# A speech joint network, forward and backward: operations recorded with reads and writes and issued by an in-kernel list scheduler; a shorter gelu'; row form of fe by DMA transpose

## The chip, the cores and the metric

One Trainium2 chip, one of its cores. The core has TensorE (PE; its weight loads are listed as PEld), VectorE (DVE), ScalarE (ACT), GpSimd (POOL) and SyncE (SP), which run their instructions in order and wait for each other by semaphores, and 16 DMA engines. SP issues all DMA transposes here; POOL issues the large loads and stores. The metric is the device time of the program in microseconds, the median of several runs.

## The reference, cut to what matters

```python
B, T, D, K, U = 2, 16000, 256, 3, 8
def _fwd_reference(x, w1, w2, g, w_f, w_g, w_o):
    xp = jnp.pad(x, ((0,0),(pad,pad),(0,0)))
    for i in range(K):
        h = h + jnp.einsum("btc,cd->btd", xp[:, i:i+T, :], w1[i])
    h = _gelu(h)[:, ::2, :]
...
    for i in range(K):
        f = f + jnp.einsum("btc,cd->btd", hp[:, i:i+T1, :], w2[i])
    f = _gelu(f)[:, ::2, :]
    fe = jnp.einsum("btd,de->bte", f, w_f)
    ge = jnp.einsum("bud,de->bue", g, w_g)
    j = jnp.tanh(fe[:, :, None, :] + ge[:, None, :, :])
    return jnp.einsum("btud,dv->btuv", j, w_o)
```

All is bfloat16, gelu is the tanh form. The outputs are this result (2 x 4,000 x 8 x 256) and the gradients of all seven inputs for a given `grad_out`.

## The kernel before

Of every four time steps of x the strided convolutions keep one of f, so the kernel works on 4,000 positions of each of two batches, in 18 chunks: 14 of 512 positions, two of 256 and two of 160. Channels lie on the 128 partitions in two halves; the four phases of x come transposed from HBM as tiles XC.

Each chunk goes through three stages, and the main loop runs stage j of chunk k beside stage a of chunk k+1 and stage de of chunk k-1:

- *Stage a* (`stage_a`): two convolutions give h at odd and even steps (HTo, HTe), a third gives f (FT). Each keeps its gelu' (G1o, G1e, G2) for the backward pass. `conv_gelu` does the six matmuls of each channel half, `gelu_half` lets ACT take the square and the gelu out of PSUM and DVE form g_s; `gelu_grad` forms gelu' with one ACT tanh and six DVE passes (lines 231 to 237). HTo is also written by DVE with the last column of the chunk before (line 274, from HTo_halo); there is one buffer of HTo. Then DMA transposes on SP make the row forms HRo, HRs, HRe and FR; fe is computed twice on PE, with channels on partitions (FE, line 309) and with positions on partitions (FER, line 322), both copied by ACT.
- *Stage j* (`stage_j`): for each pair of the eight u, ACT forms JT, the tanh of FE plus a column of GE (line 340). PE multiplies JT by WO (line 433), ACT copies the result to OUT_SB and POOL stores it. PE multiplies the transposed grad_out (GOT) by WO transposed (line 399), DVE multiplies by 1 - JT squared (JSQ, NGZ, line 411) and adds over u (ZS, line 417). The row form of the same tanh (JR: DVE adds FER and GEB, line 376; ACT, line 424) is multiplied by rows of grad_out (GO_R) into GWO_ps (line 353).
- *Stage de* (`stage_de`): backward through w_f, w2 and w1 (GF, GHo, GHe), their row forms by PE transposes and copies, the weight gradients (line 545, added to ACC by DVE, line 482), and the gradient of x (line 576), copied by ACT to GX_SB (three buffers) and stored by POOL (line 586).

Stages are generators; the main loop steps them by fixed fractions, and the framework's own scheduler gives the final order. PSUM has two pools, four banks for stage j (psj) and three for a and de (psa). Most copies out of PSUM have their engine written in the code, ACT for OUT_SB and GX_SB.

Of the kernel before, what the change touches and what calls it, by code (L numbers as in the profile page):

```python
# [17 lines left out]
GELU_A = float(2.0 * np.sqrt(2.0 / np.pi))  # L18


@with_exitstack
def kernel(
# [29 lines left out]

    CW = 512
    UP = U // 2
    full = [CW] * ((MQ - 2 * P) // CW)
# [9 lines left out]
    NG = len(chunks)  # L65

    const = ctx.enter_context(tc.tile_pool(name="const", bufs=1))
    accp = ctx.enter_context(tc.tile_pool(name="accp", bufs=1))
    xcp = ctx.enter_context(tc.tile_pool(name="xcp", bufs=7))
    htp = ctx.enter_context(tc.tile_pool(name="htp", bufs=2))  # L70
    keep = ctx.enter_context(tc.tile_pool(name="keep", bufs=3))
    fep = ctx.enter_context(tc.tile_pool(name="fep", bufs=1))
    gel = ctx.enter_context(tc.tile_pool(name="gel", bufs=2))
    jtp = ctx.enter_context(tc.tile_pool(name="jtp", bufs=3))
    gop = ctx.enter_context(tc.tile_pool(name="gop", bufs=3))
    jop = ctx.enter_context(tc.tile_pool(name="jop", bufs=2))
    jrp = ctx.enter_context(tc.tile_pool(name="jrp", bufs=3))
    keep2 = ctx.enter_context(tc.tile_pool(name="keep2", bufs=2))
    jzp = ctx.enter_context(tc.tile_pool(name="jzp", bufs=4))
    dep = ctx.enter_context(tc.tile_pool(name="dep", bufs=1))  # L80
    dep2 = ctx.enter_context(tc.tile_pool(name="dep2", bufs=2))
    x5p = ctx.enter_context(tc.tile_pool(name="x5p", bufs=4))
    gxp = ctx.enter_context(tc.tile_pool(name="gxp", bufs=3))
    psG = ctx.enter_context(tc.tile_pool(name="psG", bufs=1, space=bass.MemoryType.PSUM))
    psJ = ctx.enter_context(tc.tile_pool(name="psJ", bufs=4, space=bass.MemoryType.PSUM))
    psA = ctx.enter_context(tc.tile_pool(name="psA", bufs=3, space=bass.MemoryType.PSUM))

    def ps_j(dt=FP32):
        return psJ.tile([P, CW if dt == FP32 else 2 * CW], dt, name="psj" if dt == FP32 else "psjb", tag="psj")

    def ps_a(dt=FP32):
        return psA.tile([P, CW if dt == FP32 else 2 * CW], dt, name="psa" if dt == FP32 else "psab", tag="psa")

    def after(later, earlier, sync=True):

        cls = mybir.DependencyClass.Sync if sync else mybir.DependencyClass.NoSync
        tc.add_manual_dep(later.ins, earlier.ins.name, mybir.DependencyInfo(cls, mybir.DependencyReason.DATA),
                          reason="order of the first loads")

    xq = x.rearrange("b (q four) d -> b four q d", four=4)  # L100

    def load_xc(g_):
        b, ci, c0, W = chunks[g_]
        tiles = []
        for c in (1, 2, 3, 0):
            XC = xcp.tile([P, KT, CW + 16], BF16, name="XC")
            if c == 3 and ci > 0:
                nc.sync.dma_start_transpose(out=XC[:, :, 0:16 + W], in_=xq[b, c, c0 - 16:c0 + W, :])
            else:
                if c == 3:  # L110
                    nc.vector.memset(XC[:, :, 0:16], 0.0)
                nc.sync.dma_start_transpose(out=XC[:, :, 16:16 + W], in_=xq[b, c, c0:c0 + W, :])
            tiles.append(XC)
        return {1: tiles[0], 2: tiles[1], 3: tiles[2], 0: tiles[3]}

    def load_got(g_, up):
        b, ci, c0, W = chunks[g_]
        GOT = gop.tile([P, 2, KT, CW], BF16, name="GOT")
        for j in range(2):
            nc.sync.dma_start_transpose(out=GOT[:, j, :, :W], in_=grad_out[b, c0:c0 + W, 2 * up + j, :])  # L120
        return GOT

    def load_gor(g_, up):
        b, ci, c0, W = chunks[g_]
        GO = gop.tile([P, CW // P, 2, V], BF16, name="GO_R")
        nb, rem = W // P, W % P
        src = grad_out[b, c0:c0 + W, 2 * up:2 * up + 2, :].rearrange("t u v -> t (u v)")
        if nb:
            i_ = nc.gpsimd.dma_start(out=GO[:, 0:nb].rearrange("p a u v -> p a (u v)"),  # L129
                                     in_=src[0:nb * P].rearrange("(a p) n -> p a n", p=P))  # L130
            if g_ == 0:
                late.append(i_)
        if rem:
            nc.gpsimd.dma_start(out=GO[:rem, nb].rearrange("p u v -> p (u v)"), in_=src[nb * P:W])
        return GO

    ident = const.tile([P, P], BF16, name="ident")
    make_identity(nc, ident[:])
    W1 = const.tile([P, KK, KT, D], BF16, name="W1")
    xc_tiles = {0: load_xc(0)}  # L140
    for i in range(KK):
        nc.scalar.dma_start(out=W1[:, i], in_=w1[i].rearrange("(kt p) n -> p kt n", p=P))
    W2 = const.tile([P, KK, KT, D], BF16, name="W2")
    WF = const.tile([P, KT, D], BF16, name="WF")
# [23 lines left out]

    gTs = []

    def make_geb(b):

        for u2 in range(UP):
            ps = ps_j()
# [439 lines left out]
    for _ in gen:  # L614
        pass
# [106 lines left out]
```

## Time and profile before

| | |
|---|---|
| runs (3), median | 927.06 us (925.51 to 930.01) |
| profiled execution, span from first to last instruction | 926.7 us |
| TensorE clock, mean granted | 0.974 |
| DMA moved | 173.21 MB, mean 187 GB/s |

The profiled execution is told by its span; no other time of it is given. Its span lies 0.4 us below the median of the runs. In the profile a row of a group gives the line, engine, operation, output and inputs, shape and count; behind the bar the busy time in us, the mean ns of one, and the idle time of the engine just before them with what ended it. In the timeline a row begins with start and length in us, and idle time stands in brackets with its releaser. One name can stand for a helper: the copies of many tiles are all line 205 (ACT) or 207 (DVE).

### The profile page before, as it was taken

How to read it: one execution, taken by the hardware profiler on the slowest of the kernel's cores; microseconds unless marked ns; L12 is line 12 of the kernel's file. 1: busy time of each engine (PE TensorE's matmuls, PEld its weight loads, DVE VectorE, ACT ScalarE, POOL GpSimd, SP SyncE). 2: the span in 40 equal slices, each digit the busy share in tenths (PEclk: the TensorE clock that was granted, in tenths of full speed). 3: DMA queues.
4: the chain of work that ended last, by engine and by line, in shares of the span. 5: the costliest groups of instructions: out<-in, count | busy, mean ns of one | idle time of the engine just before them, and what ended most of it. 6: DMA issues, size and time to landing. Idle time of an engine off the chain costs nothing.

```text
span 926.7 us, 17730 instructions
## 1 busy us (share of the span) xinstructions
PE 854.3 (92%) x6396; PEld 598.7 (65%) x6396; DVE 776.6 (84%) x1807; ACT 745.6 (80%) x1271; POOL 207.2 (22%) x376
## 2 busy tenths in 40 slices
PE   5758999999999999999999999999999989899997
PEld 3434656767575766767675657576675747678873
DVE  2676999797988969897979899897979879798783
ACT  2777997979889797978697888979797897978752
POOL 2102211213122121313231212122131211214240
PEclk8888999999999999999999999999999999999997
DMA  8799998877878787785989886998887787837542
GB/s 185 124 193 217 205 239 166 241 174 208 207 178 215 169 215 174 208 204 176 187 194 213 194 189 157 233 185 228 166 230 181 163 202 173 222 109 216 144 127 67
DMA packets 308056, 173.21 MB, mean 187 GB/s; under 512 B 279648, under 2 KB 283776, under 8 KB 307968
## 3 DMA queue, kind: packets, MB, share of 16 engines
q1 hardware_dynamic: 276944, 68.48, 43.5%
q0 software_dynamic: 29152, 102.69, 34.2%
q10 hardware_dynamic: 1872, 0.92, 0.5%
q8 instruction: 50, 0.82, 0.4%
q14 instruction: 38, 0.31, 0.1%
HBM read 54.44 MB, written 50.34 MB: 113 GB/s over the span
## 4 chain that ended last, share of the span: by engine, by line
ACT 30%; PE 29%; DVE 15%; issue 15%; DMA 6%; SPq 2%; POOL 2%; ACTq 0%; POOLq 0%; DVEq 0%
ACT JT L340 9%; PE psa L545 7%; ACT JR L424 5%; ACT OUT_SB L205 5%; PE psa L576 4%; PE GWO_ps L353 4%; DMA out_dram<-GX_SB 3%; PE psj L433 3%; ACT JSQ L408 3%; PE psj L399 3%; PE psa L248 3%; DVE NGZ L411 2%; DVE ZS L417 2%; ACT g_sq L225 2%; ACT g_s L231 1%
## 5 line engine op out<-in xcount | busy, mean ns | idle before, releaser
L205 ACT CAST OUT_SB<-psj 128x512 bf16<-128x512 f32 (+1 forms) x256 | 156.9, 614 | 43.7 <-PE psj L433 43.7
L340 ACT ACTIVATE JT<-FE,GE 128x512 bf16<-128x512 f32 (+2 forms) x288 | 186.1, 700 | 0.0
L433 PE MATMUL psj<-WO,JT 128*128 128x256 bf16 (+1 forms) x1024 | 162.4, 274 | 11.3 <-ACT OUT_SB L205 10.2
L399 PE MATMUL psj<-GOT,WOT 128*128 128x512 bf16 (+2 forms) x576 | 159.8, 357 | 9.6 <-DMA GOT<-in_grad_out_dram 9.3
L411 DVE SCALAR_TENSOR_TENSOR NGZ<-JSQ,psj 128x512 f32<-128x512 bf16 (+2 forms) x252 | 152.6, 613 | 16.1 <-PE psj L399 15.9
L424 ACT ACTIVATE JR<-JR 128x1024 bf16<-128x1024 bf16 (+2 forms) x136 | 140.9, 1039 | 10.7 <-DVE JR L376 10.7
L353 PE MATMUL GWO_ps<-GO_R,JR 128*128 128x256 bf16 (+1 forms) x1024 | 144.7, 274 | 5.1 <-ACT JR L424 4.1
L433 PEld LDWEIGHTS <-JT 128*128 128x128 bf16 (+1 forms) x1024 | 99.3, 98 | 71.6 <-issue 21.0
L417 DVE TENSOR_TENSOR ZS<-ZS,NGZ 128x512 f32<-128x512 f32 (+2 forms) x216 | 131.9, 617 | 0.6
L444 POOL DMA_DIRECT2D out_dram<-OUT_SB x72 | 52.9, 735 | 315.8 <-ACT OUT_SB L205 301.5
L353 PEld LDWEIGHTS <-JR 128*128 128x128 bf16 (+1 forms) x1024 | 98.0, 98 | 30.9 <-ACT JR L424 10.4
L225 ACT ACTIVATE g_sq<-psa 128x512 bf16<-128x512 f32 (+2 forms) x106 | 60.4, 570 | 64.8 <-PE psa L248 60.7
L248 PE MATMUL psa<-XC,W 128*128 128x512 bf16 (+2 forms) x420 | 94.1, 357 | 11.9 <-DVE g_s L227 11.5
L248 PEld LDWEIGHTS <-W 128*128 128x128 bf16 x648 | 62.5, 99 | 60.9 <-issue 17.4
L482 DVE TENSOR_TENSOR ACC_GW<-ACC_GW,psa 128x512 f32<-128x512 f32 x96 | 65.6, 686 | 41.1 <-PE psa L545 41.1
L376 DVE TENSOR_TENSOR JR<-FER,GEB 128x1024 bf16<-128x1024 bf16 (+2 forms) x136 | 88.8, 657 | 9.9 <-PE GWO_ps L353 9.8
L205 ACT CAST GX_SB<-psa 128x512 bf16<-128x512 f32 (+1 forms) x128 | 76.0, 633 | 21.6 <-DMA out_dram<-GX_SB 14.3
L227 DVE SCALAR_TENSOR_TENSOR g_s<-g_sq,psa 128x512 bf16<-128x512 bf16 (+2 forms) x106 | 65.5, 618 | 29.9 <-ACT HTo L226 27.0
L545 PEld LDWEIGHTS <-X 128*128 128x128 bf16 (+1 forms) x768 | 75.0, 98 | 16.4 <-issue 3.7
L129 POOL DMA_DIRECT2D GO_R<-in_grad_out_dram x72 | 52.5, 730 | 123.7 <-PE GWO_ps L353 108.4
L399 PEld LDWEIGHTS <-WOT 128*128 128x128 bf16 x576 | 55.1, 99 | 31.3 <-DMA GOT<-in_grad_out_dram 9.9
L576 PE MATMUL psa<-W1T,GHo 128*128 128x256 bf16 (+1 forms) x384 | 74.6, 277 | 0.3
(138 smaller groups left out, 1474.8 us busy)
## 6 DMA issues: line engine op xcount, KB each, us to landing
GO_R<-in_grad_out_dram POOLq DMA_DIRECT2D x56, 512.0 KB, 5.1
out_dram<-OUT_SB POOLq DMA_DIRECT2D x56, 512.0 KB, 4.3
X<-in_x_dram POOLq DMA_DIRECT2D x60, 320.0 KB, 4.3
out_dram<-GX_SB POOLq DMA_DIRECT2D x60, 256.0 KB, 3.9
GOT<-in_grad_out_dram SPq DMA_TRANSPOSE x144, 4.7
GO_R<-in_grad_out_dram POOLq DMA_DIRECT2D x8, 256.0 KB, 5.0
out_dram<-OUT_SB POOLq DMA_DIRECT2D x8, 256.0 KB, 4.5
XC<-in_x_dram SPq DMA_TRANSPOSE x72, 4.0
```

What stands on the lines that cost most here:

```text
L205: nc.scalar.copy(out=out, in_=in_)
L248: mm = nc.tensor.matmul(ps[:, :W], lhsT=w[:, mt * P:(mt + 1) * P], rhs=rhs, start=(k == 0), stop=(k == len(mms) - 1))
L340: nc.scalar.activation(out=JT[:, j, mt, :W], in_=st[g_]["FE"][mt][:, :W], func=ACT.Tanh, bias=GE[:, b, mt, 2 * up + j:2 * up + j + 1], sca ...
L353: nc.tensor.matmul(GWO_ps[:, dt, :], lhsT=JR[:m, tb % 2, j, dt * P:(dt + 1) * P], rhs=GO[:m, tb, j, :], start=(n == 0), stop=(n == n_gwo - 1))
L376: nc.vector.tensor_tensor(out=JR[:m, lo % 2:lo % 2 + n], in0=st[g_]["FER"][:m, lo:hi].unsqueeze(2).to_broadcast([m, n, 2, D]), in1=GEB[:m, ...
L399: mm = nc.tensor.matmul(gj[:, :W], lhsT=WOT[:, kt, dt * P:(dt + 1) * P], rhs=GOT[:, j, kt, :W], start=(kt == 0), stop=(kt == KT - 1))
L411: nc.vector.scalar_tensor_tensor(out=NGZ[:, :W], in0=JSQ[:, dt, :W], scalar=1.0, in1=gj[:, :W], op0=ALU.subtract, op1=ALU.mult, accum_out= ...
L417: nc.vector.tensor_tensor(out=S["NGFE"][:, dt, :W] if fin_ else ZS[:, dt, :W], in0=ZS[:, dt, :W], in1=NGZ[:, :W], op=ALU.add)
L424: nc.scalar.activation(out=dst, in_=dst, func=ACT.Tanh)
L433: nc.tensor.matmul(ps[:m, jj * V:(jj + 1) * V], lhsT=JT[:, jj, kt, tb * P:tb * P + m], rhs=WO[:, kt, :], start=(kt == 0), stop=(kt == KT - 1))
L545: nc.tensor.matmul(ps[:, dt * D:(dt + 1) * D], lhsT=lhs(bl, m, dt), rhs=rhs[:m, bl, :], start=(k == 0), stop=(k == n - 1))
L576: nc.tensor.matmul(ps[:m, cj * D:(cj + 1) * D], lhsT=l_, rhs=r_, start=(k == 0), stop=(k == len(mms) - 1))
```

## The change

Operations are no longer issued as the code runs. Each is recorded by `op` with its engine (or a choice of ACT and DVE), a cost in ns, the buffers that it reads and writes and a place in the intended sequence; at the end `issue` simulates the engines with these costs and issues the operation that can start first, and among equals the one with the lowest place. The framework keeps that order (`manual_schedule`). With it:

- all seven PSUM banks of the two pools are one pool; a buffer is given to the operation that starts first. HTo, GF, NGFE, the row tiles and FE have two buffers (FE is bfloat16), XC six instead of seven;
- copies out of PSUM (OUT_SB, GX_SB, FE, row forms, GEB) and JSQ go to ACT or DVE, whichever the plan finds free first;
- what is kept is gelu' - 1 = (1 - t) (c (3 q + 1) h - 1/2) instead of gelu' (t the tanh, q the scaled square, h the gelu): five DVE passes instead of six, two products instead of three tensor-tensor passes; its users add the 1 in a `scalar_tensor_tensor`. GF no longer takes a factor of -1; the sign is undone where GX is copied and the weight gradients are stored;
- FER is no longer a matmul: SP transposes FE by DMA;
- the halo columns of HTo and G1o are copied by POOL, without the small HTo_halo tile;
- W2 comes in three loads, and the loads of the head are no longer held back to the first matmuls by explicit dependences.

```diff
+    WAKE = {"PE": 45.0, "ACT": 25.0, "DVE": 25.0, "POOL": 280.0, "SP": 60.0}
+    TAIL = {"PE": 180.0, "ACT": 130.0, "DVE": 95.0, "POOL": 40.0, "SP": 0.0}
...
+    def issue(self):
...
+                for o in lst:
+                    s = o.ready + wake
+                    for b in o.new:
...
+                        s = max(s, f + wake)
...
+                    k = (max(s, t), o.prio, o, e)
+                    if cand is None or k < cand:
+                        cand = k
+                if cand is not None and (best is None or cand[0] < best[0]):
+                    best = cand
...
+            T[e] = s + o.cost[o.eng.index(e)]
+            if o.work:
+                dma_free = max(dma_free, T[e] - 400.0) + o.work
+                o.done = dma_free + 2000.0
+            else:
+                o.done = T[e] + self.TAIL[e]
+            o.fn(e)
...
+def c_pe(ns):
+    return sum(max(n / 2.4 + 2.5, 25.0) for n in ns)
+def c_act(n, psum=False, ptr=False):
+    return (50.0 if psum else 93.0) + (92.0 if ptr else 0.0) + 0.833 * n
+def c_dve(n, f=1.0):
+    return 66.0 + 1.042 * n * f
...
-    psJ = ctx.enter_context(tc.tile_pool(name="psJ", bufs=4, space=bass.MemoryType.PSUM))
-    psA = ctx.enter_context(tc.tile_pool(name="psA", bufs=3, space=bass.MemoryType.PSUM))
+    F.cls("ps", 7, any_order=True, psum=True)
...
-        nc.vector.tensor_scalar(out=sq, in0=sq, scalar1=3.0, scalar2=1.0, op0=ALU.mult, op1=ALU.add)
-        nc.vector.tensor_scalar(out=om, in0=th, scalar1=-c, scalar2=c, op0=ALU.mult, op1=ALU.add)
-        nc.vector.tensor_tensor(out=om, in0=om, in1=sq, op=ALU.mult)
-        nc.vector.tensor_tensor(out=om, in0=om, in1=h, op=ALU.mult)
-        nc.vector.tensor_scalar(out=th, in0=th, scalar1=0.5, scalar2=0.5, op0=ALU.mult, op1=ALU.add)
-        nc.vector.tensor_tensor(out=gp_out, in0=om, in1=th, op=ALU.add)
+            out=sq[:, :, :W], in0=sq[:, :, :W], scalar1=3.0 * c, scalar2=c, op0=ALU.mult, op1=ALU.add),
+            out=sq[:, :, :W], in0=sq[:, :, :W], in1=h_ap(None), op=ALU.mult), r=[sq, (h_buf, 0), (h_buf, 1)], w=[sq], at=late)
+            out=sq[:, :, :W], in0=sq[:, :, :W], scalar1=-0.5, scalar2=None, op0=ALU.add), r=[sq], w=[sq], at=late)
+            out=s[:, :, :W], in0=s[:, :, :W], scalar1=-1.0, scalar2=1.0, op0=ALU.mult, op1=ALU.add),
+            out=g_ap(), in0=s[:, :, :W], in1=sq[:, :, :W], op=ALU.mult), r=[s, sq], w=[(g_buf, 0), (g_buf, 1)], at=late)
...
-                    nc.tensor.matmul(ps[:m, (bl % 2) * D:(bl % 2 + 1) * D], lhsT=FT[:, kt, bl * P:bl * P + m],
-                                     rhs=WF[:, kt, :], start=(kt == 0), stop=(kt == KT - 1))
+            dma("SP", lambda kt=kt: FER[:, 0:Wp // P, kt * P:(kt + 1) * P], lambda kt=kt: FE[:, kt, 0:Wp],
+                r=[(FE, kt), (FE, "z")], w=[(FER, kt)], bytes_=Wp * P * 2, new=[FER] if kt == 0 else [], transpose=True)
...
-            nc.vector.tensor_copy(out=HTo[:, :, 1:2], in_=pv["HTo_halo"][:])
+            op("POOL", 200.0, lambda e: nc.gpsimd.tensor_copy(out=HTo[:, :, 1:2], in_=pv["HTo"][:, :, pw + 1:pw + 2]),
...
+    ctx.enter_context(tc.manual_schedule())
+    F.issue()
```

What the order becomes, at three places. The first is ACT in a full chunk in the middle, from the copy of the last FE to the next chunk's row tanh JR. Before:

```order
L205 COPY FE_4079<-psa 128x512
L205 COPY FE_4084<-psa 128x512
L205 CAST OUT_SB<-psj 128x512
L408 ACTIVATE JSQ<-JT 128x1024
L205 CAST GX_SB<-psa 128x512
L205 CAST FER<-psa 128x512
L205 CAST OUT_SB<-psj 128x512
L205 CAST FER<-psa 128x512
L340 ACTIVATE JT<-FE_4079,GE 128x512
L205 CAST GX_SB<-psa 128x512 x3
L424 ACTIVATE JR<-JR 128x1024
```

And in the change:

```order
L276 CAST FE<-ps 128x512 x2
L517 ACTIVATE JT<-FE,GE 128x512 x2
L276 CAST OUT_SB<-ps 128x512
L517 ACTIVATE JT<-FE,GE 128x512 x3
L276 CAST OUT_SB<-ps 128x512
L517 ACTIVATE JT<-FE,GE 128x512
L565 ACTIVATE JSQ<-JT 128x1024
L517 ACTIVATE JT<-FE,GE 128x512 x2
L276 CAST OUT_SB<-ps 128x512 x2
L565 ACTIVATE JSQ<-JT 128x1024
L535 ACTIVATE JR<-JR 128x1024 x2
```

The FER copies are gone, eight tanh of JT stand ahead of the first JR, and some copies of GX_SB and OUT_SB of this stretch are on DVE. The second place is SP at the end of stage a of a full chunk: HR and FR are row forms for the weight gradients, GOT the transposed grad_out. Before:

```order
L301 DMA_TRANSPOSE FR<-FT 128x4x128
L301 DMA_TRANSPOSE HRe<-HTe 128x4x128 x2
L301 DMA_TRANSPOSE HRs<-HTo 128x4x128 x2
L301 DMA_TRANSPOSE HRo<-HTo 128x4x128 x2
L301 DMA_TRANSPOSE FR<-FT 128x4x128
L120 DMA_TRANSPOSE GOT<-in_grad_out_dram 128x2x512 x4
```

And in the change:

```order
L291 DMA_TRANSPOSE GOT<-in_grad_out_dram 128x2x512
L291 DMA_TRANSPOSE FR<-FT 128x4x128
L291 DMA_TRANSPOSE GOT<-in_grad_out_dram 128x2x512
L291 DMA_TRANSPOSE FER<-FE 128x4x128
L291 DMA_TRANSPOSE FR<-FT 128x4x128
L291 DMA_TRANSPOSE GOT<-in_grad_out_dram 128x2x512
L291 DMA_TRANSPOSE FER<-FE 128x4x128
L291 DMA_TRANSPOSE GOT<-in_grad_out_dram 128x2x512 x2
```

The two FER transposes stand each behind a load of GOT, where the loads of a group stood together. The third is POOL near the end of stage de of a full chunk; GX_SB holds the gradient of x, GHe_halo one column for the next chunk. Before:

```order
L533 COPY GHe_halo<-GHe 128x2
L444 DMA out_dram<-OUT_SB 128x4x512
L129 DMA GO_R<-in_grad_out_dram 128x4x512
L444 DMA out_dram<-OUT_SB 128x4x512
L586 DMA out_dram<-GX_SB 128x1024 x3
```

And in the change:

```order
L722 COPY GHe_halo<-GHe 128x2
L293 DMA out_dram<-OUT_SB 128x4x512
L293 DMA GO_R<-in_grad_out_dram 128x4x512
L293 DMA out_dram<-GX_SB 128x1024 x2
L293 DMA out_dram<-OUT_SB 128x4x512
L293 DMA out_dram<-GX_SB 128x1024 x2
```

Two stores of GX_SB moved ahead of the store of OUT_SB that all of them stood behind.

1169 lines of the change are left out of this document (670 added, 499 removed).

## The prediction

> **What bounds the kernel now.** I read the page's first part, then the stretches of the span, then the matmul groups by shape, and last single waits in the chain of waits and the timeline.
>
> ```profile
> PE 854.3 (92%) x6396; PEld 598.7 (65%) x6396; DVE 776.6 (84%) x1807; ACT 745.6 (80%) x1271; POOL 207.2 (22%) x376
> 430.24 3.49 PE psa L545 x32
> 176.91 1.29 PE psa L248 x6
> L433 PE MATMUL psj<-WO,JT 128*128 128x256 bf16 x992 | 157.2, 274 | 11.3 <-ACT OUT_SB L205 10.2 <-DVE NGZ L411 0.2
> ...
> L186 PE MATMUL psab<-ident,GR 8*128 8x8 bf16 x4 | 0.4, 173 | 3.3 <-DMA GR<-in_g_dram 3.3
> ```
>
> TensorE is the bound, but 92% says too much: a mean of 274 ns overlaps its successor. Where nothing waits, 32 matmuls of 256 columns take 3.49 us, 109 ns each, and six of 512 columns 1.29 us, 216 ns each. That is columns / 2.4 + 2.5 ns. Put on all shapes of the list (its first row and its last are shown), the 6,396 matmuls need **794.1 us**, a mean of 0.1242 us. Weight loads hide behind them. The execution's span is 926.7 us, so 132.6 us are lost; the stretches say where.
>
> ```profile
> 0.00:25.00 25.00, 12.27 (x76) 8.70 (x77) 6.08 (x24) 6.26 (x16) 6.92 (x19) 0.81 0.84 174
> 25.00:50.00 25.00, 19.16 (x112) 11.65 (x112) 18.21 (x52) 18.74 (x37) 2.94 (x4) 0.85 0.82 149
> 50.00:75.00 25.00, 17.07 (x89) 10.02 (x89) 17.69 (x52) 18.52 (x33) 5.14 (x8) 0.80 0.96 186
> 75.00:100.00 25.00, 18.84 (x122) 11.71 (x120) 19.19 (x42) 21.03 (x34) 3.87 (x6) 0.93 1.11 214
> 100.00:150.00 50.00, 46.66 (x333) 31.29 (x332) 48.65 (x105) 44.43 (x72) 9.35 (x16) 1.00 1.00 219
> 600.00:700.00 100.00, 96.26 (x733) 68.59 (x732) 86.84 (x185) 84.78 (x136) 21.44 (x37) 1.00 0.86 202
> 900.00:927.00 27.00, 22.01 (x128) 11.36 (x125) 9.73 (x30) 6.60 (x14) 2.08 (x4) 0.74 0.20 58
> ```
>
> A row gives a stretch's length, busy time and count of PE, weight loads, DVE, ACT and POOL, then the granted clock, the DMA share and GB/s. The first 100 us hold 399 matmuls, worth 49.5 us: 50.5 lost, in the **head**. The last 27 us hold 128, worth 15.9: 11.1 lost, in the **tail**. The 800 us between hold 5,869, worth 728.9: **71.1 lost in the middle**, 9%.
>
> In the middle PE stands mostly for an accumulator buffer that ACT or DVE has not emptied yet:
>
> ```profile
> PE psa L248 <- DVE g_s L227: 11.9, 11, 1.4
> PE psj L433 <- ACT OUT_SB L205: 10.2, 13, 1.6
> PEld L353 <- ACT JR L424: 10.4, 16, 2.1
> ...
> 741.17 2.55 ACT L340 ACTIVATE JT<-FE,GE 128x512 bf16<-128x512 f32 x4
> 743.72 0.47 ACT OUT_SB L205
> 738.91 0.94 ACT JSQ L408
> 744.25 0.60 PE L433 MATMUL psj<-WO,JT 128*128 128x256 bf16 x4 [1.57 <-ACT OUT_SB L205]
> ```
>
> The first three are rows of waits (total, times, longest), the others of the timeline and of the chain. At 742 us PE wants a buffer whose evacuation stands on ACT behind four tanh; PE loses 1.57 us. So it goes once in most chunks: 11 + 13 such waits, 22.1 us. That is a matter of order, not of load.
>
> **The change part by part.** *Work.* The row form of fe was 128 matmuls:
>
> ```profile
> L322 PE MATMUL psa<-WF,FT 128*128 128x256 bf16 x124 | 19.0, 278 | 0.6
> L234 DVE TENSOR_TENSOR g_om<-g_om,g_sq 128x1024 bf16<-128x1024 bf16 x42 | 28.9, 688 | 0.0
> 752.32 0.68 DVE L227 SCALAR_TENSOR_TENSOR g_s<-g_sq,psa 128x512 bf16<-128x512 bf16 x1
> 752.92 0.69 DVE L417 TENSOR_TENSOR ZS<-ZS,NGZ 128x512 f32<-128x512 f32 x1
> L205 ACT CAST FER<-psa 128x512 bf16<-128x512 f32 x30 | 18.9, 638 | 0.7 <-PE psa L322 0.7
> FR<-FT SPq DMA_TRANSPOSE x36, 2.9
> GOT<-in_grad_out_dram SPq DMA_TRANSPOSE x144, 4.7
> 21.39 2.48 SPq L301 DMA_TRANSPOSE HRo<-HTo  x2
> q1 hardware_dynamic: 276944, 68.48, 43.5%
> q0 software_dynamic: 29152, 102.69, 34.2%
> HBM read 54.44 MB, written 50.34 MB: 113 GB/s over the span
> ```
>
> 128 x 0.109 = **14.0 us off PE**, leaving 780.1. DVE instructions follow each other every 0.60 us. The shorter gelu' drops one product in each of 54 places, 42 of them 1024 wide: 42 x 0.60 + 12 x some 0.3 = 29 us. The counts of the changed order give it other work back: 51 GX and 46 full OUT evacuations come to DVE (97 x 0.60 = 58 us), while 39 of the large JSQ squares go to ACT (23 us less), ten large row copies as well (6 us less). With the rest, DVE stays where it is within 5 us. ACT loses the FER copies (15 us) and those 97 evacuations at 0.47 each (46 us), and takes 39 squares at 0.94 (37 us) and ten row copies (10 us): some 14 us less. So no engine gets heavier; neither DVE nor ACT ends later than PE, and their savings by themselves are worth nothing.
>
> *DMA.* 72 transposes of FE are added, of the size of FR<-FT: 2 x 4,000 x 256 x 2 bytes = 4.1 MB on q1. At q1's own pace (43.5% of the span for 68.48 MB) that is 24 us of all 16 engines, and 72 issues of SP at 1.24. Before, the two queues' packets fill 77.7% of the span; afterwards, in 877 us, 85%.
>
> *Order.* ACT, DVE and PE rows are now placed by a plan of durations in which a buffer is taken from one pool of seven accumulator banks instead of pools of three and four, and an evacuation may go to whichever of ACT and DVE is free first. The numbers in the plan stand close to rows of this trace: 109 ns for a matmul of 256, 599 ns for a DVE pass of 512, against the 109 and 600 above. So I expect its order to hold on the chip. I credit it with the two buffer waits (22.1 us) and with the wait for JR (10.4, PE's weight loads): 32 of the 71.1, so 39 stay. Bounds: nothing gained, 71; and all but 15 gained, since some wait stays in every stretch.
>
> The stores of GX show how such a stall starts on POOL:
>
> ```profile
> 726.78 0.76 POOL L444 DMA_DIRECT2D out_dram<-OUT_SB  x1 [10.70 <-ACT OUT_SB L205]
> 728.36 0.56 POOL L586 DMA_DIRECT2D out_dram<-GX_SB  x1 [0.83 <-ACT GX_SB L205]
> 734.56 0.59 ACT L205 CAST GX_SB<-psa 128x512 bf16<-128x512 f32 x1 [3.11 <-DMA out_dram<-GX_SB]
> ```
>
> A GX store stands behind an OUT store that waits 10.70 us for ACT, and ACT then waits 3.11 us for the GX buffer. Now two GX stores go ahead of that OUT store. ACT gets up to 3 us per chunk; PE had cover for it, so I count nothing.
>
> *Head.* DVE waited 12.1 us there to write the halo of the next chunk into the single HTo buffer, which transposes still read, and PE 9.3 us behind it:
>
> ```profile
> 27.68 0.17 DVE L274 COPY HTo<-HTo_halo 128x2 bf16<-128x2 bf16 x1 [12.12 <-DMA HRs<-HTo]
> 28.22 0.37 PE L309 MATMUL psa<-FT,WF 128*128 128x256 bf16 x1 [9.31 <-DVE g_s L227]
> 68.11 1.03 PE L399 MATMUL psj<-GOT,WOT 128*128 128x512 bf16 x2 [6.22 <-DMA GOT<-in_grad_out_dram]
> 12.03 0.21 PE L186 MATMUL psab<-ident,GR 8*128 8x8 bf16 x2 [3.30 <-DMA GR<-in_g_dram]
> ```
>
> HTo has two buffers now and the halo copy is POOL's: the 9.3 us go. What is late next is GOT by DMA (6.22 us at 68 us), with the DMA share at 0.82 to 1.11. Against it, ACT's first row is now the GEB copy, which needs g; in the trace g was used at 12.0 us, after the convolutions that it now precedes. With g loaded first I put 2.6 us on it (0 to 4). Queued behind it are all gelu of chunk 0. FER by transpose comes some 3 us later than its copy did, while ACT has 16 tanh of chunk 0 ahead of JR; nothing. Head: 50.5 - 9.3 + 2.6 = 43.8 if nothing else is late, 53 if GOT takes it all back; I take 47.
>
> The granted clock in the head's rows is 0.80 to 0.93; at 0.85 the head's 49.5 us of matmuls take 8.7 us longer than at full speed. I leave these in the sum, since the gap of GOT's kind stays. The Trainium skill, "TensorE: Matmul & The Clock Gate" (HAM oscillation), says that idle gaps of more than about 3.4 us make the clock drop again. By that rule a head without such gaps would save these 8.7 us too, and the sum would be 869; the trace agrees in that the low clock lies where the gaps of 9.31 and 6.22 us lie, and no row of it shows the head without them.
>
> *Sum.* 780.1 + 47 + 39 + 11.1 = **877.2 us** of span; the median of the runs is 927.06, 0.4 above this span, so **877.5 us**. The tail is unchanged in kind.
>
> **Rivals.**
>
> *The transposes bind* (0.15). More DMA in less time: 177.3 MB, of which 18.1 in the head (174, 149, 186 and 214 GB/s, 25 us each) and 1.6 in the tail. If the middle's 157.6 MB run at no more than the 202 GB/s of the 600 to 700 row, it takes 780 us, and the kernel 780 + 97 + 27 = **904**. Against it: 219 GB/s at share 1.00 was held from 100 to 150 us, which would allow 720. For it: PE's waits for GOT (6.22 us at 68 us) stand where the share is near 1. The HBM row shows 113 GB/s. The Trainium skill, "Perfetto Trace Analysis" (Identifying the Most-Contended Engine), would have DMA judged by such HBM use and not by the share, which it calls misleading with 16 engines. By that rule this rival falls away and 877 stays; the trace speaks against it with the waits for GOT just named.
>
> *Order is worth nothing* (0.13). The waits only change names, and the removed work is all: 780.1 + 50.5 + 70 + 11.1 = **912**. For it: four resources at 78 to 92% leave little slack in a fixed order.
>
> *The change does not shorten PE's path* (0.05): the work goes, waits fill it, **927**.
>
> *FER arrives late in every chunk: slower* (0.09). A pair's JR, on which GWO_ps hangs, now needs a transpose behind GOT loads in SP's queue, and these wait for PE:
>
> ```profile
> SPq L120 <- PE psj L433: 155.8, 27, 11.3
> ```
>
> Between the FE copy and the first JR ACT has eight tanh, four OUT copies and two squares, 8 x 0.64 + 4 x 0.47 + 2 x 0.94 = 8.9 us. Two issues (2.5) and a landing (2.9) fit, with 3.5 us to spare. If a GOT load ahead waits the longest 11.3 us, JR is 7.8 us late; ACT stands in order, and OUT evacuations and PE behind it. In half of 16 chunk periods that is 62 us, in all 125: **940** to 1002. It decides from 3.1 us per chunk (50 / 16). Against it: the mean of those 27 waits is 5.8 us, and where SP waits for PE it has loaded ahead.
>
> **How the numbers follow.** The forecast has 0.58, with its own range 842 (15 us left in the middle, 37 in the head) to 895. Beyond it lie DMA-bound (904), no order (912), no gain (927) and slower (940 on). 842 to 922 leaves about 0.14 above and 0.05 below. A measurement of this kernel can tell some 0.5%, 4.6 us, from no change: faster 0.58 + 0.15 + 0.13 = 0.86, same 0.05, slower 0.09.
>
> **What would show it.** Right: PE's count of matmuls 128 lower; the 9.3 us gap at 28 us gone; waits of PE for g_s and OUT_SB evacuations well under 22 us; 100 us of the middle carrying over 94 us of full-rate matmuls; ACT waits for a GX store gone. Wrong: waits of ACT or DVE for FER, or of PE for GOT, of some us in every chunk; a DMA share at 1 through the middle; GOT landing far over 4.7 us. The weakest numbers are the 32 us credited to the order and the head.

## The result, and the profile after

The changed kernel takes **903.76 us** (median; 899.67 to 921.28) where the kernel before took 926.28 beside it. The ratio is 0.974 (95%: 0.970 to 0.978): 2.6% faster, where 5.3% was forecast. The profiled execution took 899.67 us, with a span of 897.9. Single executions of one kernel spread by 2 to 3% (six more of this one 891.7 to 916.9, eleven of before beside them 918.1 to 938.3); the ratios below leave disturbed executions out, the medians don't, and where a5's profile would stand in the next table, d4's does, since a5's was disturbed.

First come the page's busy times, its two large queues, its HBM row and the chain by engine, for the changed kernel:

```profile
PE 836.3 (93%) x6268; PEld 585.4 (65%) x6268; DVE 776.8 (87%) x1748; ACT 738.3 (82%) x1191; POOL 215.9 (24%) x412
...
q1 hardware_dynamic: 294480, 72.67, 50.1%
q0 software_dynamic: 29152, 102.69, 40.3%
HBM read 54.44 MB, written 50.34 MB: 117 GB/s over the span
...
PE 56%; DVE 19%; DMA 11%; ACT 9%; issue 3%; SPq 2%; ACTq 0%; DVEq 0%
```

The 128 matmuls are gone. VectorE is busy for the same time as before (776.6), now at 87% of the span. The chain has moved from ACT (30% before, 9% now) to TensorE, and DMA has 11% of it (6% before). Three stretches follow, with the columns as in the prediction's table of stretches, then single waits of PE and DVE (total, times, longest) and, in the last row, the FER transposes from issue to landing:

```profile
0.00:100.00 100.00, 69.10 (x417) 42.51 (x418) 64.01 (x167) 65.52 (x112) 19.85 (x42) 0.88 0.84 171
100.00:200.00 100.00, 87.53 (x582) 56.01 (x580) 81.09 (x164) 77.00 (x118) 18.31 (x35) 0.95 0.97 200
200.00:800.00 600.00, 587.38 (x4458) 414.88 (x4457) 553.26 (x1184) 530.34 (x825) 146.03 (x270) 1.00 0.96 209
...
PE ps L268 <- DVE g_s L382: 7.1, 16, 1.0
PE ps L268 <- ACT OUT_SB L276: 3.2, 7, 0.7
PE GWO L268 <- ACT JR L535: 10.9, 9, 4.0
PE ps L268 <- ACT GEB L276: 11.5, 1, 11.5
...
DVE JR L528 <- DMA FER<-FE: 10.5, 7, 4.6
DMA to landing us min/median/max: 2.8/5.9/14.1
```

The two buffer waits of the forecast fell from 22.1 to 10.3 us. GWO's wait for JR, which the forecast took off too, grew instead: 4.1 us of PE and 10.4 of its weight loads before, 10.9 and 15.3 now, and JR waits for a transpose that before did not exist. One wait of 11.5 us, for the copy of GEB on ACT, is new in the head. Counting the matmuls of a stretch form by form at full rate (columns / 2.4 + 2.5 ns), what each stretch loses is, in us, for profiles whose matmul records are complete:

| profiled execution | 0 to 100 | 100 to 200 | 200 to 800 | span |
|---|---|---|---|---|
| before | 48.5 | 8.0 | 54.3 | 926.7 |
| changed | 47.3 | **21.3** | 34.8 | 897.9 |
| before, shorter gelu' alone (b1) | 46.7 | 14.1 | 32.1 | 902.9 |
| before, FER by transposes alone (b2) | 68.4 | 14.7 | 65.4 | 959.7 |
| scheduler alone (a7) | 43.4 | 11.3 | 31.3 | 893.0 |
| best version in another order (d4) | 38.2 | 7.3 | 27.6 | 880.2 |

So in this execution most of what the middle loses beyond the forecast lies between 100 and 200 us. Some 4 us of those 21.3 go with the clock: the stretch's 78.7 us of matmuls at the granted 0.95 take 4.1 us longer than at 1.00, which before's row from 100 to 150 us has. The place is a matter of the order: c1 below, the same kernel with a few instructions moved, loses 16.8 us there and 43.7 from 200 to 800. The chain has these pieces there (start, length, what):

```profile
89.20 7.45 DMA HRe<-HTe
116.33 10.55 DMA GOT<-in_grad_out_dram
179.16 11.37 DMA FER<-FE
190.56 0.70 DVE JR L528
191.29 1.06 ACT JR L535
```

The last three rows are the new path: a FER transpose that takes 11.37 us to land, then JR on VectorE, then its tanh; GWO on TensorE comes next. In the head one stall took the place of another. ACT's timeline, changed kernel (start, length, instruction, idle time before it and its releaser):

```profile
3.15 10.87 ACTq L293 DMA_DIRECT2D W<-in_w_dram  x4
20.69 0.37 ACTq L293 DMA_DIRECT2D WF<-in_w_f_dram  x1
21.11 1.07 ACT L276 CAST GEB<-ps 128x512 bf16<-128x512 f32 x2 [18.41 <-DMA W<-in_w_dram]
22.07 0.40 ACT L378 ACTIVATE g_sq<-ps 128x256 bf16<-128x256 f32 x1
...
7.32 13.35 DMA GOT<-in_grad_out_dram
```

The last row is of the chain: a GOT transpose lands at 20.67 us and releases ACT's load of WF at 20.69. In the trace's records the two are given the same semaphore, 110: the load waits until the transpose before it on that semaphore has landed. So it is this program's sharing of semaphores that ties ACT to SP's transposes. ACT computes nothing until these loads are issued; in the kernel before its first gelu square ran at 7.9 us, here at 22.07.

### The profile page after: what moved, and what is told of

It reads as the page before. It is cut to its first block, busy times and chain, and to the rows that moved or that the text cites. A ratio compares the mean times of both kernels' runs of the same rounds, so it can differ in the third digit from the quotient of the medians.

```text
span 897.9 us, 17416 instructions
## 1 busy us (share of the span) xinstructions
PE 836.3 (93%) x6268; PEld 585.4 (65%) x6268; DVE 776.8 (87%) x1748; ACT 738.3 (82%) x1191; POOL 215.9 (24%) x412
## 3 DMA queue, kind: packets, MB, share of 16 engines
q1 hardware_dynamic: 294480, 72.67, 50.1%
q0 software_dynamic: 29152, 102.69, 40.3%
## 4 chain that ended last, share of the span: by engine, by line
PE 56%; DVE 19%; DMA 11%; ACT 9%; issue 3%; SPq 2%; ACTq 0%; DVEq 0%
PE ps L268 46%; PE GWO L268 8%; DMA FER<-FE 7%; DVE NGZ L575 3%; DMA GOT<-in_grad_out_dram 3%; DVE JR L528 3%; DVE ZS L583 2%; DVE g_s L382 2%; SPq L291 2%; ACT OUT_SB L276 2%; PE psb L624 2%; ACT JSQ L565 1%; ACT g_sq L378 1%; ACT JR L535 1%; DVE ACC L647 1%
## 5 line engine op out<-in xcount | busy, mean ns | idle before, releaser
L517 ACT ACTIVATE JT<-FE,GE 128x512 bf16<-128x512 bf16 (+2 forms) x288 | 178.5, 672 | 0.3 <-DVE FE L281 0.2
L276 ACT CAST OUT_SB<-ps 128x512 bf16<-128x512 f32 (+1 forms) x207 | 121.7, 592 | 64.3 <-PE ps L268 63.7
L268 PE MATMUL ps<-GOT,WOT 128*128 128x512 bf16 (+2 forms) x576 | 154.0, 352 | 12.6 <-DVE g_s L382 4.4
L575 DVE SCALAR_TENSOR_TENSOR NGZ<-JSQ,ps 128x512 f32<-128x512 bf16 (+2 forms) x252 | 153.4, 614 | 13.9 <-PE ps L268 13.1
L268 PE MATMUL ps<-WO,JT 128*128 128x256 bf16 (+1 forms) x1024 | 154.6, 275 | 7.1 <-DVE NGZ L575 1.4
L268 PE MATMUL GWO<-GO_R,JR 128*128 128x256 bf16 (+1 forms) x1024 | 134.9, 277 | 10.9 <-ACT JR L535 10.9
L565 ACT ACTIVATE JSQ<-JT 128x1024 bf16<-128x1024 bf16 (+2 forms) x119 | 114.3, 960 | 16.6 <-DVE NGZ L575 15.6
L268 PEld LDWEIGHTS <-JR 128*128 128x128 bf16 (+1 forms) x1024 | 99.3, 99 | 37.1 <-ACT JR L535 15.3
L382 DVE SCALAR_TENSOR_TENSOR g_s<-g_sq,ps 128x512 bf16<-128x512 bf16 (+2 forms) x108 | 66.4, 616 | 41.4 <-ACT HTo L380 27.0
L528 DVE TENSOR_TENSOR JR<-FER,GEB 128x1024 bf16<-128x1024 bf16 (+2 forms) x136 | 87.2, 657 | 10.7 <-DMA FER<-FE 10.5
L268 PE MATMUL ps<-ROWS,X 128*128 128x256 bf16 (+1 forms) x768 | 95.9, 273 | 0.5 <-DVE NGZ L575 0.4
L268 PE MATMUL ps<-XC,W 128*128 128x512 bf16 (+2 forms) x432 | 92.5, 361 | 2.1 <-DVE GHo L698 0.8
```

Of the source, the lines that this page charges most:

```text
L268: nc.tensor.matmul(ps_ap, lhsT=lhsT, rhs=rhs, start=start, stop=stop)
L276: nc.scalar.copy(out=dst(), in_=src())
L382: op("DVE", c_dve(W), lambda e, mt=mt, ps=ps: nc.vector.scalar_tensor_tensor(out=s[:, mt, :W], in0=sq[:, mt, :W], scalar=1.0, in1=ps[:, :W ...
L517: op("ACT", c_act(W, ptr=True), lambda e, j=j, mt=mt: nc.scalar.activation(out=JT[:, j, mt, :W], in_=S["FE"][:, mt, :W], func=ACT.Tanh, bi ...
L528: op("DVE", c_dve(n * 2 * D, 0.5), lambda e, lo=lo, n=n, m=m, JR=JR: nc.vector.tensor_tensor(out=JR[:m, lo % 2:lo % 2 + n], in0=S["FER"][: ...
L565: nc.scalar.activation(out=JSQ[:, :, :W], in_=JT[:, j, :, :W], func=ACT.Square)
```

## The experiments

Eighteen kernels ran. Two of them repeat the changed kernel, as itself and with a meaningless change of order, to say what a difference is worth. All times are medians, all ratios against the kernel before on the same chip.

| kernel | us | ratio (95%) |
|---|---|---|
| b1: before, shorter gelu' | 904.0 | 0.972 (0.968 to 0.977) |
| b2: before, FER by DMA | 958.0 | 1.030 (1.025 to 1.035) |
| b4: before, one PSUM pool of 7 | 937.6 | 1.011 (1.007 to 1.015) |
| d2: b1 and one product more | 920.1 | 0.994 (0.991 to 0.998) |
| d3: before, gelu' in another order | 920.0 | 0.992 (0.989 to 0.995) |
| a7: scheduler alone | 903.5 | 0.970 (0.965 to 0.975) |
| a3: changed, gelu' of before | 910.0 | 0.973 (0.964 to 0.981) |
| a2: changed, FER by matmuls | 892.7 | 0.964 (0.960 to 0.968) |
| c0: changed, again | 902.7 | 0.967 (0.961 to 0.973) |
| c1: changed, wake 50 for 45 ns | 912.3 | 0.974 (0.969 to 0.980) |
| a1: changed, W2 and WF by POOL | 894.3 | 0.964 (0.959 to 0.969) |
| a4: changed, landing 4500 ns | 896.0 | 0.966 (0.961 to 0.971) |
| d1: a2 and transposes nobody reads | 899.7 | 0.966 (0.960 to 0.972) |
| d5: a1 and FER first in SP's queue | 902.6 | 0.973 (0.965 to 0.981) |
| d6: d5 and landing 3500 ns | 891.1 | 0.964 (0.957 to 0.971) |
| **a5: a1 and a2** | **885.6** | **0.955 (0.950 to 0.960)** |
| a6: a5 and landing 4500 ns | 890.7 | 0.962 (0.958 to 0.967) |
| d4: a5, wake 50 for 45 ns | 886.1 | 0.957 (0.952 to 0.962) |

### What a difference is worth: c0, c1

```diff
-    WAKE = {"PE": 45.0, "ACT": 25.0, "DVE": 25.0, "POOL": 280.0, "SP": 60.0}
+    WAKE = {"PE": 50.0, "ACT": 25.0, "DVE": 25.0, "POOL": 280.0, "SP": 60.0}
```

> The changed kernel once more, unchanged, for the spread between runs and for a ratio on the same chip as the next three. All theories: 0.974 of before, 900 to 906; single executions from 895 to 920.

> Changed kernel, where the list scheduler counts 50 ns instead of 45 for TensorE to wake: a change without a meaning of its own, which moves a few instructions past each other and alters no transfer, no queue and no count of instructions. If the gains of the head, FER and landing experiments (8 to 10 us each) have the causes that they were made for, this one gives 0 to 3 us either way, 900 to 906. Rival (any other order differs by as much, so that those gains are the luck of an order): 890 to 898 or 908 and more.

The same kernel measured 0.974 and 0.967; the order without a meaning 0.974. The latter came out 9.6 us above c0 by the medians, against an expectation of 3, so up to 1% can be the luck of a run or of an order. JR's wait for FER is part of that luck: 9.1 us in c0's profile, and in c1's

```profile
DVE JR L528 <- DMA FER<-FE: 18.9, 5, 9.8
```

So an edit of one part of the changed kernel has to be read with its waits, or from several runs together.

### The three parts alone: b1, b2, a7

b1 takes the five VectorE instructions for gelu' into the kernel before (with the plus one and the signs where the value is used), b2 only the transposes of FE, a7 is the changed kernel without these two.

```diff
-        nc.vector.tensor_scalar(out=sq, in0=sq, scalar1=3.0, scalar2=1.0, op0=ALU.mult, op1=ALU.add)
-        nc.vector.tensor_scalar(out=om, in0=th, scalar1=-c, scalar2=c, op0=ALU.mult, op1=ALU.add)
-        nc.vector.tensor_tensor(out=om, in0=om, in1=sq, op=ALU.mult)
-        nc.vector.tensor_tensor(out=om, in0=om, in1=h, op=ALU.mult)
-        nc.vector.tensor_scalar(out=th, in0=th, scalar1=0.5, scalar2=0.5, op0=ALU.mult, op1=ALU.add)
-        nc.vector.tensor_tensor(out=gp_out, in0=om, in1=th, op=ALU.add)
+        nc.vector.tensor_scalar(out=sq, in0=sq, scalar1=3.0 * c, scalar2=c, op0=ALU.mult, op1=ALU.add)
+        nc.vector.tensor_tensor(out=sq, in0=sq, in1=h, op=ALU.mult)
+        nc.vector.tensor_scalar(out=sq, in0=sq, scalar1=-0.5, scalar2=None, op0=ALU.add)
+        nc.vector.tensor_scalar(out=th, in0=th, scalar1=-1.0, scalar2=1.0, op0=ALU.mult, op1=ALU.add)
+        nc.vector.tensor_tensor(out=gp_out, in0=th, in1=sq, op=ALU.mult)
...
```

> Kernel before, with only the shorter gelu' (five VectorE instructions for six, 16-bit products two for three, and the plus one put back where the value is used). My forecast's step (VectorE's load is worth nothing by itself): 922 to 930. Rival (VectorE's 29 us less come off where it is waited for, 15% of the chain and more): 900 to 918.

904.0: the rival. One part alone, in the kernel before, gives as much as the whole change. The page and waits of b1:

```profile
PE 843.2 (93%) x6396; PEld 598.8 (66%) x6396; DVE 749.7 (83%) x1753; ACT 747.8 (83%) x1277; POOL 215.2 (24%) x376
...
PE psa L247 <- DVE g_s L227: 4.8, 10, 0.7
PE psj L432 <- ACT OUT_SB L205: 1.3, 4, 0.4
```

VectorE has 27 us less, and the same two buffer waits that the forecast had called "a matter of order, not of load" are down from 22.1 to 6.1 us. The order in the code is otherwise that of before; the framework's scheduler, which gives the final order there, shifted some instructions too (4,212 of TensorE's 6,396 matmuls have the same tiles at the same place in the order as before, 5,881 in d2 below).

Now b2, where the FER matmuls and their copies are gone:

```diff
...
+            nc.sync.dma_start_transpose(out=FER[:, 0:Wp // P, kt * P:(kt + 1) * P], in_=S["FE"][kt][:, 0:Wp])
```

> Kernel before, with only FER by two DMA transposes of FE (FE in 16 bits then); 128 matmuls less, 14.0 us at full rate. Theory 2 (what the transposes' landings hold, JR and GWO, costs as much as the matmuls did or more): 920 to 935, with JR waiting for its FER by 10 us or more in all. Rival (the landings are covered, TensorE's work comes off): 908 to 916.

958.0, beyond the upper end: 30 us lost for 14 us of matmuls taken away. Waits of DVE, ACT and SP's queue in b2, and its FER transposes from issue to landing:

```profile
DVE JR L371 <- DMA FER<-FE: 76.0, 12, 19.6
ACT JR L419 <- DVE JR L371: 59.7, 20, 17.2
SPq L120 <- PE psj L428: 129.2, 31, 14.3
...
DMA to landing us min/median/max: 2.3/5.5/7.5
```

VectorE stands in front of the JR until the transpose has landed, and ACT behind it: the forecast's slower rival, 12 times and by up to 19.6 us. No landing took over 7.5 us, so the longest of these waits are not the landing alone; as that rival had it, the transposes stand in SP's queue, whose GOT loads (line 120) wait for TensorE by up to 14.3 us.

> Changed kernel, with FER by matmuls and the six-instruction gelu': the scheduler alone, with the computation of before. If the order carries the gain and the transposes give 10 us of it back: 889 to 899. Rival (the shorter gelu' is what the scheduler lives on, VectorE being at 88%): 905 to 920.

903.5, between the two: the scheduler alone gives 24 us, as gelu' alone does. Together (a2) they give 34, not 48. Of the two buffer waits the scheduler alone takes one: PE's wait for OUT_SB copies on ACT is down to 0.9 us, but the other, 11.9 us at line 248 before, is not shorter (one line now stands for all matmuls):

```profile
PE ps L268 <- DVE g_s L382: 13.3, 21, 1.3
```

With the shorter gelu' on top it is 8.6 us in a2 and 7.1 in the changed kernel.

### Load or order of gelu's steps: d2, d3

d2 adds one line to b1, a product that nobody reads; d3 has as many steps as before, with the product by h moved ahead of the tanh's result:

```diff
+        nc.vector.tensor_tensor(out=om, in0=th, in1=sq, op=ALU.mult)
```

```diff
-        nc.vector.tensor_scalar(out=sq, in0=sq, scalar1=3.0, scalar2=1.0, op0=ALU.mult, op1=ALU.add)
-        nc.vector.tensor_scalar(out=om, in0=th, scalar1=-c, scalar2=c, op0=ALU.mult, op1=ALU.add)
+        nc.vector.tensor_scalar(out=sq, in0=sq, scalar1=3.0 * c, scalar2=c, op0=ALU.mult, op1=ALU.add)
+        nc.vector.tensor_tensor(out=sq, in0=sq, in1=h, op=ALU.mult)
+        nc.vector.tensor_scalar(out=om, in0=th, scalar1=-1.0, scalar2=1.0, op0=ALU.mult, op1=ALU.add)
         nc.vector.tensor_tensor(out=om, in0=om, in1=sq, op=ALU.mult)
-        nc.vector.tensor_tensor(out=om, in0=om, in1=h, op=ALU.mult)
```

> Kernel before with the shorter gelu', and one more 16-bit product after it into a tile that nobody reads: VectorE's load of before, the order of steps of after. If the load is what the shorter gelu' takes away: 918 to 929. Rival (the order: three of the five steps don't need the tanh and run while ACT makes it): 901 to 909.

> Kernel before, with its six VectorE instructions for gelu' in another order: the two that don't need the tanh first, so that one more of them runs while ACT makes it; as many instructions and as much time on VectorE as before. If the load decides: 920 to 930. Rival (the order of steps): 902 to 912.

Both lie where the load was to decide, at its edge. d2 puts the load back and keeps the new order of steps: 16 of the 24 us are gone (904.0 to 920.1). d3 changes the order alone and gains 7.6. So about two thirds of b1 are load and a third the order of steps (four fifths and one fifth by the ratios); what the framework's own shifts add to either is not told apart.

### Buffers: b4

```diff
-    psJ = ctx.enter_context(tc.tile_pool(name="psJ", bufs=4, space=bass.MemoryType.PSUM))
-    psA = ctx.enter_context(tc.tile_pool(name="psA", bufs=3, space=bass.MemoryType.PSUM))
+    psJ = ctx.enter_context(tc.tile_pool(name="psJ", bufs=7, space=bass.MemoryType.PSUM))
...
-        return psA.tile([P, CW if dt == FP32 else 2 * CW], dt, name="psa" if dt == FP32 else "psab", tag="psa")
+        return ps_j(dt)
```

> Kernel before, with one PSUM pool of seven in place of four and three, in the same order of instructions. My forecast's middle term put 22.1 us on waits for a PSUM buffer. If the split of the pools makes them, they go without the scheduler: 903 to 912. Rival (they come from the order, in which the engine that frees a buffer is late whoever owns it): 920 to 930.

Slower, beyond either. The two buffer waits are nearly gone, and another is in their place:

```profile
PE psj L432 <- ACT OUT_SB L204: 1.1, 3, 0.6
PE GWO_ps L352 <- ACT JR L423: 36.8, 14, 3.9
```

TensorE gets a buffer sooner and stands before GWO instead, for 36.8 us where it was 4.1. Read so, its wait for a buffer had covered a lateness of ACT and VectorE and not caused one; since the framework's scheduler also moved instructions on ACT in b4, this is an argument and not shown by itself.

### FER in the changed kernel: a2, a3, d1, d5, d6

```diff
-            dma("SP", lambda kt=kt: FER[:, 0:Wp // P, kt * P:(kt + 1) * P], lambda kt=kt: FE[:, kt, 0:Wp],
...
+            op("PE", c_pe([D] * (KT * len(bls))), fmm, r=[(FT, 0), (FT, 1), WF], w=[ps], new=[ps] + ([FER] if h == 0 else []))
+            for lo, hi, m in groups(bls):
+                evac(lambda lo=lo, hi=hi, m=m: FER[:m, lo:hi].rearrange("p a d -> p (a d)"),
```

> Changed kernel, with FER made by matmuls of FT and WF again (128 more on TensorE, 14 us at full rate) and written out of PSUM by whichever of ACT and DVE the scheduler takes; no DMA transposes of FE. Theory 2 (the landings of the FER transposes, 5.9 us in the median and up to 11.4, hold JR and GWO and cost most of the 21.3 us lost in 100:200): the 14 us come back as shorter waits, loss in 100:200 falls to 8 to 12, the time is 897 to 906. Rival (the FER landings are covered; TensorE's work decides): 14 us of work more and 912 to 920.

892.7, below the range: TensorE does 14 us more, and by the medians the kernel is 10 to 11 us faster than c0 and the changed one (0.3 to 1.0% by the ratios). The same exchange gives 9 us from a1 to a5 and 6 from a3 to a7: three pairs that differ in this alone, all one way, though each by itself is about as large as the step from c0 to c1 or smaller. GWO's wait for JR falls from 10.9 us to

```profile
PE GWO L268 <- ACT JR L544: 3.9, 6, 1.7
```

> Changed kernel, with gelu' less one made by six VectorE instructions instead of five (the steps of before, one more 16-bit product and one more tile), about 29 us more of VectorE work in all; nothing else. My forecast's step (VectorE's load is worth nothing by itself): 901 to 908. Rival (VectorE at 87% of the span is the next bound, and the shorter gelu' carries the gain): 915 to 932, with VectorE busy over 800 us.

910.0, with an interval of 15 us: between the two theories. On top of the scheduler the shorter gelu' is worth 6 to 11 us by the medians (a3 against changed, a7 against a2) and nothing to 0.6% by the ratios, where it was worth 24 us, 2.8%, in the kernel before. a3's profile also has JR waiting 21.4 us for FER, so that a3 alone doesn't tell.

For d1 the transposes of FE go into a tile of their own, beside a2's matmuls:

```diff
...
+        FER2 = buf("fer2", [P, NB, D], BF16, "FER2")
+        for kt in range(KT):
+            dma("SP", lambda kt=kt: FER2[:, 0:Wp // P, kt * P:(kt + 1) * P], lambda kt=kt: FE[:, kt, 0:Wp],
...
```

> Changed kernel, with FER by matmuls, and the transposes of FE issued as well, into a tile that nobody reads. If what FER's transposes cost is the wait of JR and GWO for the landing: 889 to 897, as with the matmuls alone (892.7). Rival (they cost by standing in SP's queue and by slowing GOT and XC): 899 to 908.

899.7, which would speak for the traffic, but its interval holds both cases. Its profile has JR waiting for no transpose and 10.6 us lost from 100 to 200, as without transposes (11.3 in a7). b2 shows the wait as a cost in the order of before; how a2's gain in the scheduler's order divides between the wait and the traffic stays open.

d5 has a1's edit and the first part of this one, d6 both.

```diff
-                r=[(FE, kt), (FE, "z")], w=[(FER, kt)], bytes_=Wp * P * 2, new=[FER] if kt == 0 else [], transpose=True)
+                r=[(FE, kt), (FE, "z")], w=[(FER, kt)], bytes_=Wp * P * 2, new=[FER] if kt == 0 else [], transpose=True,
+                at=t0)
...
-                o.done = dma_free + 2000.0
+                o.done = dma_free + 3500.0
```

> Changed kernel, with W2 and WF loaded by POOL, and FER's transposes given the scheduler's rank of the chunk's first convolution, so that SP issues them ahead of GOT, HRo, HRs and HRe where they are ready. If their place in SP's queue is what they cost: 880 to 888, JR's wait for FER under 6 us (15.2 with the loads on POOL alone). Rival (the landing itself, or what the extra traffic does to the other transfers): 890 to 898.

> As the one before, and the scheduler counts 3500 ns for a landing instead of 2000. If a plan that knows the landings hides them: 878 to 888, below the best version with matmuls (885.6) by up to 7. Rival (traffic): 889 to 897.

Put first in SP's queue, the transposes gain nothing, and d5 is slower than either of its theories said. Waits of DVE and PE in d5:

```profile
DVE JR L529 <- DMA FER<-FE: 15.8, 6, 8.8
PE ps L268 <- DMA GOT<-in_grad_out_dram: 8.7, 2, 7.8
```

JR waits for FER as in a1 (15.2 us), and TensorE now for GOT too. With longer landings in the plan d6 comes to 891.1, in the range of its rival, with JR waiting 11.6 us. Neither median reaches the 885.6 of the matmuls, though d6's interval overlaps a5's.

### The start and the plan's landing: a1, a4, a5, a6, d4

```diff
-    wload("ACT", W2, i, lambda i=i: W2[:, i], lambda i=i: w2[i].rearrange("(kt p) n -> p kt n", p=P), BIG + 1)
+    wload("POOL", W2, i, lambda i=i: W2[:, i], lambda i=i: w2[i].rearrange("(kt p) n -> p kt n", p=P), BIG + 1)
-    wload("ACT", WF, 0, lambda: WF[:], lambda: w_f.rearrange("(kt p) n -> p kt n", p=P), BIG + 1)
+    wload("POOL", WF, 0, lambda: WF[:], lambda: w_f.rearrange("(kt p) n -> p kt n", p=P), BIG + 1)
```

> Changed kernel, with the loads of W2 and WF issued by POOL instead of ACT; nothing else. Theory 1 (in the changed kernel ACT stands from 3.15 to 20.69 us in its own queue behind these loads, and the first gelu square runs at 22.07 us where it ran at 7.9 before): the first square comes at 8 to 10 us, the loss in 0:100 falls from 47.3 to 34 to 40, the time from 903.8 to 889 to 897. Rival (the start is bound by the landings of XC, GOT and FER themselves, so that ACT would wait for them elsewhere): the square comes earlier but the loss in 0:100 stays at 44 or more and the time at 900 to 906.

894.3, in the range. The first square on ACT's timeline of a1:

```profile
10.37 0.38 ACT L378 ACTIVATE g_sq<-ps 128x256 bf16<-128x256 f32 x1 [7.67 <-PE ps L268]
```

It runs 11.7 us earlier, a little later than expected, and what it waits for now is the first convolution; PE's wait for GEB is gone. The head's loss, expected at 34 to 40 us, can't be counted in a1, whose matmul records are incomplete. In complete ones with this edit it is 38.2 (d4), 40.5 (d6), 40.8 (a6) and 46.2 (d5, with a 7.8 us wait for GOT in it), and 43.4 to 50.1 in those without (a7, c1, changed, c0, d1).

> Changed kernel, where the list scheduler counts 4500 ns instead of 2000 from the end of a transfer's packets to its landing; only the order of instructions follows from it. Theory 3 (the order is made for landings that are too early: GOT takes 5.4 us in the median, FER 5.9, so instructions that wait for them stand in front of others that could run): 892 to 899, loss in 100:200 under 15. Rival (the order hardly depends on it, or loses as much elsewhere): 900 to 908.

> Changed kernel, with W2 and WF loaded by POOL and FER made by matmuls again. If the two costs are separate (ACT's queue at the start, 9 us; FER's landings, 10 us), they add: 880 to 887, loss in 0:100 under 42 by the clock and chain rows, JR waiting for its FER less than 3 us in all. Rival (both are the same start-up stretch, which the one or the other shortens): 890 to 896.

> As the kernel with the two edits (W2 and WF by POOL, FER by matmuls), and the scheduler counts 4500 ns for a landing too. If the longer landing helped only through FER's (JR's wait for FER fell from 22 us to 6 in that run), it adds nothing once FER is made on TensorE: within 4 us of the kernel with two edits. Rival (it helps the loads GOT and XC by itself, 8 us): 5 to 10 us faster than that.

> The best version (W2 and WF by POOL, FER by matmuls), with the scheduler's wake of TensorE at 50 ns for 45: another order without a meaning. If its two causes carry its time: 881 to 892. Rival (its time was the luck of one order): 895 or more.

a4 changes one number in the scheduler (2000.0 to 4500.0 ns for a landing) and gives 896.0; JR's wait for FER fell from 10.5 us to 5.2 (the 22 us in a6's expectation is not a number of the trace). Once FER is on TensorE the longer landing adds nothing: a6 is 5 us slower than a5. a5 has 885.6 and beats both kernels; d4, the same with another order, 886.1: this gain outlasts the change of order. Both intervals lie below that of the changed kernel as first measured (0.970 to 0.978); against its repeat c0 (0.961 to 0.973) a5's is clear and d4's touches it. The head loses 38.2 us in d4, against 47.3; d4 has FER by matmuls too.

## Why the prediction was wrong, point by point

The step that failed is the term for the row form of fe: 14.0 us off TensorE, and "nothing" for FER's lateness. With that term taken back the forecast is 877.5 + 14.0 = 891.5; a2, the change without these transposes, measured 892.7. That the rest comes out so close is partly luck, as the points below say.

- **Work, 14.0 us off TensorE.** Right as a count, wrong as a gain. "FER by transpose comes some 3 us later than its copy did ... nothing" was the step: the transposes took 5.9 us in the median and up to 14.1 to land, and JR with GWO hangs on them. In the kernel before that costs 44 us for 14 (b2); in the scheduler's order the 14 are given back and 6 to 11 us lost besides, by the medians of three pairs. The count of 72 transposes was wrong as well: the list has 36, two per chunk, as for FR.
- **"Their savings by themselves are worth nothing."** Wrong, but it hid a gain and so can't be why the kernel was slower than forecast. VectorE's 27 us less are worth 24 in the kernel before (b1), 16 by load and 8 by the order of steps (d2, d3). That VectorE at 84% ends no later than TensorE says nothing of a stretch: it frees the PSUM buffers, late whenever an instruction stands ahead.
- **Order, 32 us.** Mechanism half right. The scheduler alone brings 24 (a7); it takes away the wait for OUT_SB (10.2 to 0.9 us), and PE's weight loads wait 4.9 us for JR where it was 10.4. The wait for g_s, 11.9 of the 22.1 called "a matter of order, not of load", stays at 13.3 and shrinks only with the lighter load; one pool without the scheduler loses 10 us (b4). The shorter gelu' removes some of the same waits, so the two add up to 34 (a2) and not to the sum of their gains, 48. That these 34 lie so near the 32 is luck: part of them is gelu's, which was counted as nothing.
- **Head, 47.** Right by two errors that cancel. The 9.3 us behind HTo went, as forecast; ACT's queue, counted at 2.6 for GEB, made PE wait 11.5 and held the first square 14 us longer. Without it, and with FER by matmuls, the head loses 38.2 (d4). The granted clock of the first 25 us was 0.77 with that stall, and 0.86 (d5) to 1.00 (d4, d6) without it.
- **Middle, 39.** With 897.9 - 780.1 = 117.8 us lost, 47.3 of it in the head and 10.8 in the last 23 us, 59.7 stay. From 200 us on the size is about as forecast (34.8 up to 800). A forecast loss spread evenly would put 5 us between 100 and 200; 21.3 are lost there, so 16 of the 20.7 us too many lie in that stretch, with the landings of HRe, GOT and FER above and the lower clock. With FER on TensorE it loses 7.3 (d4) and 11.3 (a7).
- **Tail, 11.1.** 10.8, over a shorter stretch. The forecast's split of before valued every matmul at the mean, 0.1242 us; form by form before loses 48.5 us in the head, 69.0 in the middle and some 15 in the last 27, with the same sum.
- **Rivals.** "The transposes bind" named 904, the time that came, but not by its reason: at a share of 0.96 the middle moved 209 GB/s, more than the 202 of that rival, and d6 runs 891 with all transposes. The Trainium skill, "Perfetto Trace Analysis" (Identifying the Most-Contended Engine), would judge DMA by HBM use; with 117 GB/s beside shares that rose while the kernel got faster, the trace agrees. "FER arrives late" named the path that failed; its 62 us are near b2's 76 us of waits, but the scheduler runs other work in front of JR, so that 7 waits of 10.5 us in all are left in the changed kernel, and 18.9 with another order (c1).
- **Signs.** Those of being right came: 128 matmuls fewer, no gap of 9.3 us, the two buffer waits at 10.3, no ACT wait for a GX store, and 94.1 us of full-rate matmuls from 600 to 700 (92.0 to 99.1 in the other hundreds from 200 to 800). Those of being wrong asked for waits for FER in every chunk and a DMA share of 1; 7 waits and 0.96 came. So the signs could not tell this result from the forecast.

The same section of the Trainium skill says to optimize the most contended engine first. By full-rate work TensorE is that engine (794.1 of 926.7 us). Here the runs differ: 27 us taken off the second engine made the kernel before 24 us faster (b1), while 14 us taken off TensorE made it 30 us slower (b2), though the transposes in their place brought waits of their own, so that b2 is no plain test.

## What to carry to other kernels

A wait of the bounding engine for a buffer can be the lateness of the engine that empties it: price a lighter load there at what that wait holds, even where its share of the span is far from full, and don't add it to the gain of a better order that removes the same wait. A transpose by DMA in place of a few matmuls trades 109 ns each for a landing of 2.8 to 14.1 us; do it only where nothing in a fixed order hangs on it. Before an engine that has to compute in the first microseconds issues loads, look at what the semaphores of these loads wait for.

## What the runs showed of the hardware

- The same transfers' packets took longer in another order: q0 moves the same 102.69 MB in 34.2% of 926.7 us before and 40.3% of 897.9 after, 317 and 362 us. More transfers are not needed for it: a7, with the packets and bytes of before on both queues, has 42.0% of 893.0 us, 375. The share of DMA is no measure of work done.
- ACT's load of WF, issued at 20.69 us, waited for a GOT transpose of SP's queue, landed at 20.67, whose semaphore it uses. With W2 and WF loaded by POOL the first square came at 10.37 us for 22.07.
- The landing of a FER transpose went from 2.8 to 14.1 us in one execution. The 2.8 belong to a smaller chunk; among full ones it was 3.8 to 14.1.
